# Statistics one tile ahead, earlier transposes, and the last output tile in three pieces, in a fused attention and feed-forward kernel

## The chip, the cores and the metric

The kernel runs on one core of a Trainium2 chip. The metric is the device time of one execution in microseconds (us). Before the change the median was 224.88 us (4 runs, 224.37 to 225.04). A profile shows the span of one execution, about 1.7 us shorter than its device time (223.4 against 225.12 for the profiled execution of the kernel before).

Names: PE is TensorE's matmuls and PEld its weight loads, DVE is VectorE, ACT ScalarE, POOL GpSimd, SP SyncE. "ACTq" and "SPq" are the sequencers of ACT and SP issuing DMAs. PSUM (psT in the profile) is where PE's results lie, in numbered banks, until another engine reads them.

## The reference, cut to what matters

```python
x  = A_x                                    # [1, 2048, 640], bf16
xn = (x - mean) / sqrt(var + 1e-5)          # layer norm over the 640 columns
q, k, v = split(xn @ wqkv)                  # 32 heads of 20
phi = lambda t: where(t > 0, t + 1, exp(t)) + 1e-6
kv, z = sum_s phi(k) v^T, sum_s phi(k)      # linear attention
s = (phi(q) kv / (phi(q) z + 1e-6)) @ wo
g = silu(relu(xn @ w1) @ w2)                # w1 is [640, 1728]
out = x + s * g
```

The rows come as 16 tiles of 128. Tiles 0 to 3 are transposed on PE after their mean is taken off; tiles 4 to 15 are normalised on VectorE and transposed by a DMA.

## The kernel before

A scheduler helper records operations per engine, in program order, and puts in the semaphore waits. So an engine runs its own list strictly in order, and an instruction that waits holds everything behind it. The parts that matter:

```python
def aggr(t):                                # statistics, then rsy = (var + eps)^-0.5 on POOL
    DVE: bn_aggr(mv[t], stats[t])
    POOL: rsv[t] = var + eps
    POOL: rsy[t] = rsv[t] ** -0.5
def LN_stats(t): bn(t, 0); bn(t, 1); aggr(t)
def LN_norm(t):                             # needs rsy[t]
    DVE: xn[t] = (xin[t] - mean[t]) * rsy[t]
    if t >= 4: SP: DMA transpose xn[t] -> xnT[t]
    if t + 8 < 16: SP: load tile t + 8
# K_mm(t): 10 PE matmuls into two PSUM banks, of xcT (t < 4) or xnT
# K_exp(t), K_relu(t): ACT evacuates the banks into slot t % 4 of ek
def K_fin(t):                               # frees the slot
    DVE: e = min(e, 1) + 1e-6
    DVE: pk[t] = e + r
# ... cut ...
# hidden blocks of the first 512 rows; K_mm(4) follows n = 5, K_mm(5) follows n = 7
for n in range(13):
    H_block(0, n)                           # 5 matmuls of 512 columns on PE, relu on ACT
    if n < 4:
        LN_norm(n + 4)
        if n < 3: LN_stats(n + 5)
    if n in (3, 4): K_fin(2 * n - 6); K_fin(2 * n - 5)
    if 4 <= n < 8: LN_norm(n - 4)
    # ... cut ...
    if n in {5: 4, 7: 5, 9: 6, 11: 7}:
        K_mm(t, 0); K_exp(t, 0); K_relu(t, 0); K_fin(t)     # all on banks 0 and 1
```

Two more pieces of the argument come later in the program. In the G phase, five blocks of 32 matmuls (`G_block`) use the bank pairs 0, 2, 0, 2, 4 in turn, and ACT copied each result to SBUF. Just ahead of those copies in ACT's list stand four DMA issues that load w2. At the end, each output tile is made from ten matmuls (`s_tile`), the gate `g = silu(...)` by ACT, a multiply and an add by VectorE, and a store; the last tile was done in two halves of 320 columns.

## Time and profile before

| what | value before | where it is read |
|---|---|---|
| device time, median | 224.88 us | the runs |
| PE busy | 97% of 223.4 us | page, part 1 |
| hole before K_mm(5) | PE free at 22.74, starts 24.48 | timeline of PE |
| VectorE waits for rsy | 5 waits, 5.0 us | waits |
| G phase, first matmul to first matmul after it | 112.33 to 134.31 = 21.98 us | timeline |
| gate end to last add, last add to span end | 1.71 and 2.41 us | timeline |

PE is the bound. The page of the kernel before, its head:

```profile
span 223.4 us, 3512 instructions
PE 216.8 (97%) x1442; PEld 133.8 (60%) x1442; DVE 115.0 (51%) x213; ACT 86.6 (39%) x142; POOL 45.9 (21%) x69
```

That is an average. The view by stretches says where PE is not full. Each line has the stretch, its length and the busy time of PE, PEld, DVE, ACT and POOL, each with its count; then the TensorE clock that was granted (1.00 is full speed), the DMA share and GB/s.

```profile
0.00:12.60 12.60, 11.15 (x93) 9.04 (x94) 6.61 (x22) 7.12 (x14) 3.74 (x15) 1.00 0.81 247
12.60:24.50 11.90, 10.32 (x54) 4.93 (x52) 8.65 (x23) 8.06 (x15) 5.52 (x11) 1.00 0.75 202
24.50:112.20 87.70, 87.70 (x480) 43.69 (x481) 68.94 (x108) 52.82 (x89) 33.31 (x43) 1.00 0.27 65
112.20:134.30 22.10, 22.02 (x162) 15.58 (x161) 0.00 (x0) 3.41 (x5) 0.00 (x0) 1.00 0.90 281
134.30:218.30 84.00, 84.00 (x650) 59.64 (x648) 29.26 (x58) 14.47 (x20) 3.30 (x1) 1.00 0.21 74
```

In the third and fifth stretch PE is busy all the time. The second has lost 1.6 us. VectorE's timeline there shows why (start, duration, engine, line and operation; the bracket is idle time before it and what ended it):

```profile
14.37 0.45 DVE L435 TENSOR_SCALAR reg<-reg,mv,rsy 128x640 bf16<-128x640 bf16 x1
...
16.86 0.45 DVE L435 TENSOR_SCALAR reg<-reg,mv,rsy 128x640 bf16<-128x640 bf16 x1 [1.00 <-POOL rsy L424]
...
19.34 0.45 DVE L435 TENSOR_SCALAR reg<-reg,mv,rsy 128x640 bf16<-128x640 bf16 x1 [1.00 <-POOL rsy L424]
...
21.82 0.45 DVE L435 TENSOR_SCALAR reg<-reg,mv,rsy 128x640 bf16<-128x640 bf16 x1 [1.00 <-POOL rsy L424]
...
22.54 0.49 DVE L530 TENSOR_TENSOR reg<-regE 128x640 bf16<-128x640 bf16 x1
```

L435 is `LN_norm`; three times it waits 1.00 us for POOL's rsy, whose statistics VectorE itself finished only just before. The first L530 is the end of K_fin(0), at 23.03. And PE, on the same clock:

```profile
20.58 2.32 PE L570 MATMUL psT<-regX,reg 128*128 128x512 bf16 x10
24.48 1.53 PE L495 MATMUL psT<-reg 128*128 128x320 bf16 x10 [1.58 <-ACT regE L512]
```

Ten matmuls of 512 columns take 2.16 us (0.216 each; the 2.32 printed includes a modelled end), so PE was free at 22.74. K_mm(5) needs banks 0 and 1, which K_exp(4) and K_relu(4) free; K_exp(4) needs slot 0 of `ek`, which K_fin(0) frees. ACT's timeline shows that K_exp(4) waited for it:

```profile
23.12 1.30 ACT L512 ACTIVATE regE<-psT 128x640 bf16<-128x640 f32 x2 [3.11 <-DVE reg L530]
```

The true hole is 1.74 us.

In the G phase ACT's queue is held by issuing w2. The timeline of the kernel before:

```profile
114.76 5.70 ACTq L780 DMA_DIRECT2D reg<-in_B_w_dram  x2
120.51 1.42 ACT L793 ACTIVATE reg<-psT 128x640 bf16<-128x640 f32 x2 [7.38 <-issue]
121.26 12.88 PEld L788 LDWEIGHTS psT<-reg 128*128 128x128 bf16 x96 [0.42 <-ACT reg L793]
```

The tail of the kernel before, with the gate (L868), the multiplies (L893) and the adds (L896):

```profile
218.58 0.70 ACT L868 ACTIVATE reg<-psT 128x640 bf16<-128x640 f32 x1 [5.54 <-PE psT L840]
219.38 0.49 DVE L893 TENSOR_TENSOR reg<-psT,reg 128x320 bf16<-128x320 f32 x1 [1.22 <-ACT reg L868]
219.91 0.33 DVE L896 TENSOR_TENSOR reg<-reg 128x320 bf16<-128x320 bf16 x1
220.15 0.48 DVE L893 TENSOR_TENSOR reg<-psT,reg 128x320 bf16<-128x320 f32 x1
220.67 0.32 DVE L896 TENSOR_TENSOR reg<-reg 128x320 bf16<-128x320 bf16 x1
```

### The profile page before, as it was taken

The page shows a single profiled execution, that of the slowest core. Times are in us where ns is not written, and L with a number is a line of the kernel's source. Part 1 is how long each engine was busy: PE and PEld are TensorE (multiplying, and loading weights), DVE is VectorE, ACT ScalarE, POOL GpSimd, SP SyncE. Part 2 cuts the span into 40 slices and gives each one's busy share as a digit, 9 for nine tenths or more (in the row PEclk, how much of TensorE's full clock was granted, in tenths as well). Part 3 has the DMA queues.
Part 4 walks back from the last instruction along what each step waited for, and adds up shares of the span by engine and source line. Part 5 has one row for each costly group of instructions (what it writes and reads, how often), then busy time and mean ns, then how long its engine had stood idle before and what let it go on. Part 6 is the DMA issues. An engine that isn't in the chain of part 4 may idle for free.

```text
span 223.4 us, 3512 instructions
## 1 busy us (share of the span) xinstructions
PE 216.8 (97%) x1442; PEld 133.8 (60%) x1442; DVE 115.0 (51%) x213; ACT 86.6 (39%) x142; POOL 45.9 (21%) x69
## 2 busy tenths in 40 slices
PE   8999799999999999999999999999999999999993
PEld 8655354555544555444466777677767776776672
DVE  4766996798649999783700002940424240412243
ACT  4585766656665576554412113232021102110211
POOL 2252631111041599950000005000000000000000
PEclk9999999999999999999999999999999999999999
DMA  6996389621001233000099969900010100001011
GB/s 178 283 339 130 87 248 140 190 44 29 3 1 29 59 94 115 0 0 3 11 204 321 341 245 369 323 12 3 29 59 32 59 29 32 29 29 59 3 59 60
DMA packets 27761, 23.91 MB, mean 107 GB/s; under 512 B 11873, under 2 KB 27105, under 8 KB 27745
## 3 DMA queue, kind: packets, MB, share of 16 engines
q1 hardware_dynamic: 24512, 19.50, 30.7%
q10 hardware_dynamic: 3232, 4.18, 5.4%
q8 instruction: 11, 0.18, 0.3%
q14 instruction: 6, 0.04, 0.1%
HBM read 15.81 MB, written 5.24 MB: 94 GB/s over the span
## 4 chain that ended last, share of the span: by engine, by line
PE 83%; DVE 4%; ACTq 3%; DMA 3%; SPq 2%; ACT 1%; POOL 1%; issue 1%; DVEq 0%
PE psT L840 25%; PE psT L570 21%; PE psT L548 10%; PE psT L879 9%; PE psT L495 7%; PE psT L788 6%; DMA reg<-in_A_x_dram 3%; ACTq L780 3%; DVE stats L416 2%; PE psT L817 1%; PE psT L858 1%; PE psT L587 1%; SPq L358 1%; ACTq L776 1%; POOL rsy L424 1%
## 5 line engine op out<-in xcount | busy, mean ns | idle before, releaser
L840 PE MATMUL psT<-reg,hT 128*128 128x320 bf16 x416 | 60.5, 299 | 0.0
L840 PEld LDWEIGHTS psT<-reg,hT 128*128 128x128 bf16 x416 | 40.3, 98 | 16.5 <-issue 1.1
L570 PE MATMUL psT<-reg 128*128 128x512 bf16 x195 | 46.0, 379 | 0.0
L893 DVE TENSOR_TENSOR reg<-psT,reg 128x640 bf16<-128x640 f32 (+1 forms) x17 | 13.3, 785 | 48.8 <-PE psT L879 47.6
L574 ACT ACTIVATE hT<-psT 128x512 bf16<-128x512 f32 x52 | 30.5, 601 | 17.4 <-PE psT L570 17.4
L570 PEld LDWEIGHTS psT<-reg 128*128 128x128 bf16 x195 | 18.9, 98 | 22.0 <-issue 0.4
L868 ACT ACTIVATE reg<-psT 128x640 bf16<-128x640 f32 x12 | 8.2, 702 | 43.1 <-PE psT L840 23.6
L548 PE MATMUL psT<-reg 128*128 128x512 bf16 x100 | 24.8, 379 | 0.0
L506 POOL TENSOR_TENSOR zacc<-zacc,reg 128x640 f32<-128x640 f32 x16 | 23.8, 1489 | 3.7 <-DVE reg L530 2.8
L879 PE MATMUL psT<-reg,pqT 128*128 128x320 bf16 x160 | 24.3, 299 | 0.0
L788 PE MATMUL psT<-reg 128*128 128x320 bf16 x160 | 22.1, 299 | 0.1
L512 ACT ACTIVATE regE<-psT 128x640 bf16<-128x640 f32 x24 | 15.6, 701 | 11.4 <-PE psT L495 8.3
L495 PE MATMUL psT<-reg 128*128 128x320 bf16 x120 | 18.3, 299 | 1.6 <-ACT regE L512 1.6
L788 PEld LDWEIGHTS psT<-reg 128*128 128x128 bf16 x160 | 15.6, 98 | 6.6 <-ACT reg L793 0.4
L879 PEld LDWEIGHTS psT<-reg,pqT 128*128 128x128 bf16 x160 | 15.7, 98 | 6.1
L556 DVE TENSOR_SCALAR regE<-psT 128x512 bf16<-128x512 f32 x20 | 13.6, 682 | 8.2 <-ACT regE L555 8.2
L558 DVE SCALAR_TENSOR_TENSOR pqT<-regE 128x512 bf16<-128x512 bf16 x20 | 17.4, 870 | 0.7
L548 PEld LDWEIGHTS psT<-reg 128*128 128x128 bf16 x100 | 9.8, 98 | 11.5
L495 PEld LDWEIGHTS psT<-reg 128*128 128x128 bf16 x120 | 11.7, 98 | 8.3 <-ACT regE L512 2.1
L416 DVE BATCH_NORM_STATS2 stats<-reg 128x6 f32<-128x320 bf16 x32 | 14.1, 479 | 3.3 <-DMA reg<-in_A_x_dram 3.3
L806 DVE TENSOR_TENSOR reg<-psT,mv 128x120 bf16<-128x120 f32 (+1 forms) x6 | 1.1, 261 | 27.9 <-POOL reg L910 27.9
L530 DVE TENSOR_TENSOR reg<-regE 128x640 bf16<-128x640 bf16 x16 | 14.5, 909 | 1.4 <-ACT regE L512 1.0
(68 smaller groups left out, 166.6 us busy)
## 6 DMA issues: line engine op xcount, KB each, us to landing
reg<-in_A_x_dram SPq DMA_DIRECT2D x16, 160.0 KB, 3.0
scr<-regE SPq DMA_DIRECT2D x4, 640.0 KB, 11.2
reg<-in_A_x_dram SPq DMA_DIRECT2D x4, 640.0 KB, 9.2
out_dram<-reg SPq DMA_DIRECT2D x15, 160.0 KB, 1.8
regE<-scr SPq DMA_DIRECT2D x4, 512.0 KB, 5.3
reg<-in_B_w_dram ACTq DMA_DIRECT2D x1, 1120.0 KB, 12.3
reg<-in_B_w_dram ACTq DMA_DIRECT2D x1, 1040.0 KB, 6.6
reg<-in_A_wo_dram SPq DMA_DIRECT2D x6, 160.0 KB, 4.2
```

Source lines behind the costliest of these rows:

```text
L416: sc.op("DVE", lambda eng: eng.bn_stats(stats[:, t, a, :], xv[:, HN * a:HN * (a + 1)]), R=[("xin", t % XR)], W=[("stats", t, a)])
L495: fns.append(lambda eng, a=a, k=k, lhs=lhs: eng.matmul(ps[b + a][:, 0:HN], lhsT=lhs[:, k, tok(t)], rhs=wqk[:, k, D + HN * a:D + HN * (a + 1)],
L506: sc.op("POOL", lambda eng: eng.tensor_tensor(out=zacc[:, :], in0=zacc[:, :], in1=pk[:, t, :], op=ALU.add), R=[("zacc",), ("pk", t)], W=[( ...
L512: sc.op("ACT", lambda eng: eng.activation(out=o_.rearrange("p (a n) -> p a n", a=2), in_=ps2(b, HN), func=func, scale=scale), R=[("ps", b) ...
L530: sc.op("DVE", lambda eng: eng.tensor_tensor(out=pk[:, t, :], in0=e_, in1=r_, op=ALU.add), R=[("ek_e", es), ("ek_r", es)], W=[("pk", t)])
L548: sc.group("PE", [(lambda eng, k=k: eng.matmul(ps[b], lhsT=wqk[:, k, P * f:P * (f + 1)], rhs=xnT[:, k, schunk(j)], start=(k == 0), stop=(k ...
L558: sc.op("DVE", lambda eng: eng.scalar_tensor_tensor(out=pqT[:, f, schunk(j)], in0=e_, scalar=1.0, in1=r_, op0=ALU.min, op1=ALU.add), R=[(" ...
L570: a = sc.group("PE", [(lambda eng, k=k: eng.matmul(ps[b], lhsT=w1_sb[:, k, P * f:P * (f + 1)], rhs=src[:, k, :], start=(k == 0), stop=(k = ...
L574: sc.op("ACT", lambda eng: eng.activation(out=hT[:, f, schunk(j)], in_=ps[b], func=ACTF.Relu), R=[("ps", b)], W=[("hT", j, f)])
L788: fns.append(lambda eng, t=t, a=a: eng.matmul(ps[b + a][:, 0:HN], lhsT=xn[:, t, P * k:P * (k + 1)], rhs=pk[:, t, HN * a:HN * (a + 1)], sta ...
L840: sc.group("PE", [(lambda eng, f=f: eng.matmul(ps[b][:, 0:HN], lhsT=hT[:, f, tok(t)], rhs=w2_sb[:, f, HN * n:HN * (n + 1)], start=(f == 0 ...
L879: sc.group("PE", [(lambda eng, c=c, a=a: eng.matmul(ps[b + a][:, 0:HN], lhsT=pqT[:, c, tok(t)], rhs=wf[:, c, HN * a:HN * (a + 1)], start=( ...
```

## The change

The intent is to keep PE fed at the opening, to take the rsy waits off VectorE, to free PSUM in the G phase sooner, and to overlap the last tile's work. There are four parts.

```diff
@@ opening @@
-    for k in range(KA, C):
-        K_mm(0, 2, k, k + 1)
-        K_mm(1, 4, k, k + 1)
     bn(1, 1)
     centre(2)
     aggr(1)
-    transposes(2, 0)
+    bn(2, 0)
     mean_act(3, 0)
-    bn(2, 0)
-    xcT_copy(2, 0, 0, "DVE")
-    xcT_copy(2, 0, 1, "DVE")
+    for k in range(KA, C):
+        if k == C - 1:
+            transposes(2, 0)
+            xcT_copy(2, 0, 0, "DVE")
+            xcT_copy(2, 0, 1, "DVE")
+        K_mm(0, 2, k, k + 1)
+        K_mm(1, 4, k, k + 1)
     # ... cut ...
-    bn(2, 1)
     xcT_copy(3, 0, 0, "DVE")
-    xcT_copy(3, 0, 1, "ACT")
+    xcT_copy(3, 0, 1, "DVE")
+    bn(2, 1)
     # ... cut ...
-    K_mm(3, 0)
+    K_mm(3, 0, 0, KA)
+    K_mm(3, 0, KA, C)
     K_exp(1, 4)
     K_relu(1, 4)
-    LN_stats(4)
     bn(3, 0)
     bn(3, 1)
     aggr(3)
+    LN_stats(4)
@@ first hidden blocks @@
                 if n < 4:
-                    LN_norm(n + 4)
                     if n < 3:
                         LN_stats(n + 5)
-                if n in (3, 4):
-                    K_fin(2 * n - 6)
-                    K_fin(2 * n - 5)
+                    LN_norm(n + 4)
+                if 1 <= n < 5:
+                    K_fin(n - 1)
@@ G_block @@
-        sc.op("ACT", lambda eng: eng.activation(out=GT[...], in_=ps2(b, HN), func=ACTF.Copy), ...)
+        sc.op("DVE", lambda eng: eng.tensor_copy(GT[...], ps2(b, HN)), ...)
@@ last output tile @@
+    LC = [0, 224, 432, 640]     # columns
+    LB = [2, 3, 4]              # PSUM banks
-    s_tile(pairs[7][1], 2, last=True)       # 320 + 320
+    s_last(pairs[7][1])                     # 224 + 208 + 208, each with its own mult, add and store
```

More of the change, by code (lines that the diff above doesn't have):

```diff
@@ L260, in bass_recurrent_scan__linear_attn_block__dense_activation_relu__prompt_kernel @@
     kvp = reg3[:, 0:VC * D].rearrange("p (c n) -> p c n", c=VC)
-    outb = reg3[:, VC * D:(VC + NOUT) * D].rearrange("p (a n) -> p a n", a=NOUT)
-    tmpo = reg3[:, (VC + NOUT) * D:(VC + 2 * NOUT) * D].rearrange("p (a n) -> p a n", a=NOUT)
+    NB = NOUT + 1
+    outb = reg3[:, VC * D:(VC + NB) * D].rearrange("p (a n) -> p a n", a=NB)
+    tmpo = reg3[:, (VC + NB) * D:(VC + 2 * NB) * D].rearrange("p (a n) -> p a n", a=NB)
     pqT = nc.alloc_sbuf_tensor("pqT", [P, C, S], bf)
@@ L632, in bass_recurrent_scan__linear_attn_block__dense_activation_relu__prompt_kernel @@
     K_mm(2, 6, KA, C, (1,))
+    xcT_copy(3, 0, 0, "DVE")
+    xcT_copy(3, 0, 1, "DVE")
     bn(2, 1)
-    xcT_copy(3, 0, 0, "DVE")
-    xcT_copy(3, 0, 1, "ACT")
     w1_load(2, "ACT")
@@ L792, in G_block @@
                       W=[("ps", b), ("ps", b + 1)])
-        sc.op("ACT", lambda eng: eng.activation(out=GT[:, k, :].rearrange("p (a n) -> p a n", a=2), in_=ps2(b, HN),
-                                                func=ACTF.Copy), R=[("ps", b), ("ps", b + 1)], W=[("GT", k)])
+        sc.op("DVE", lambda eng: eng.tensor_copy(GT[:, k, :].rearrange("p (a n) -> p a n", a=2), ps2(b, HN)),
+              R=[("ps", b), ("ps", b + 1)], W=[("GT", k)])
         return ag
@@ L872, in bass_recurrent_scan__linear_attn_block__dense_activation_relu__prompt_kernel, with s_out @@
     so = [0]
-    def s_tile(t, b, last=False):
+    LC = [0, 224, 432, 640]
+    LB = [2, 3, 4]
+    def s_out(t, os_, i, lo, hi, src, keys, na):
+        shp = "p (a n) -> p a n"
+        sc.op("DVE", lambda eng: eng.tensor_tensor(
+            out=tmpo[:, os_, lo:hi].rearrange(shp, a=na), in0=src, in1=g_sb[:, t, lo:hi].rearrange(shp, a=na),
+            op=ALU.mult), R=keys + [("g", t)], W=[("tmpo", os_, i)])
+        sc.op("DVE", lambda eng: eng.tensor_tensor(out=outb[:, os_, lo:hi], in0=tmpo[:, os_, lo:hi],
+                                                   in1=xre[:, t, lo:hi], op=ALU.add),
+              R=[("tmpo", os_, i), ("xre", t // 4)], W=[("outb", os_, i)])
+        dma("SP", lambda eng: eng.dma_start(out2[tok(t), lo:hi], outb[:, os_, lo:hi]), R=[("outb", os_, i)])
@@ L875, in s_tile, with s_mm @@
+    def s_mm(t, lo, hi, b):
+        i = t // 4
+        sc.group("PE", [(lambda eng, c=c: eng.matmul(
+            ps[b][:, 0:hi - lo], lhsT=pqT[:, c, tok(t)], rhs=wf[:, c, lo:hi],
+            start=(c == 0), stop=(c == C - 1))) for c in range(C)],
+            R=[("pqT", i, c) for c in range(C)] + [("wf", c) for c in range(C)], W=[("ps", b)])
+    def s_tile(t, b):
         os_ = so[0] % NOUT
         so[0] += 1
-        i = t // 4
         for a in range(2):
-            sc.group("PE", [(lambda eng, c=c, a=a: eng.matmul(
-                ps[b + a][:, 0:HN], lhsT=pqT[:, c, tok(t)], rhs=wf[:, c, HN * a:HN * (a + 1)],
-                start=(c == 0), stop=(c == C - 1))) for c in range(C)],
-                R=[("pqT", i, c) for c in range(C)] + [("wf", c) for c in range(C)], W=[("ps", b + a)])
@@ L884, in piece @@
-        def piece(lo, hi, pin, addE="DVE"):
-            shp = "p (a n) -> p a n"
-            na = 2 if pin is None else 1
-            src = ps2(b, HN) if pin is None else ps[pin][:, 0:HN].unsqueeze(1)
-            def kk(nm):
-                return [(nm, os_, h) for h in (0, HN) if lo <= h < hi]
-            keys = [("ps", b), ("ps", b + 1)] if pin is None else [("ps", pin)]
-            sc.op("DVE", lambda eng: eng.tensor_tensor(
-                out=tmpo[:, os_, lo:hi].rearrange(shp, a=na), in0=src, in1=g_sb[:, t, lo:hi].rearrange(shp, a=na),
-                op=ALU.mult), R=keys + [("g", t)], W=kk("tmpo"))
-            sc.op(addE, lambda eng: eng.tensor_tensor(out=outb[:, os_, lo:hi], in0=tmpo[:, os_, lo:hi],
-                                                      in1=xre[:, t, lo:hi], op=ALU.add),
-                  R=kk("tmpo") + [("xre", t // 4)], W=kk("outb"))
-            dma("SP", lambda eng: eng.dma_start(out2[tok(t), lo:hi], outb[:, os_, lo:hi]), R=kk("outb"))
@@ L901, in s_tile, with s_last @@
-        if last:
-            piece(0, HN, b)
-            piece(HN, D, b + 1)
-        else:
-            piece(0, D, None)
+            s_mm(t, HN * a, HN * (a + 1), b + a)
+        s_out(t, os_, 0, 0, D, ps2(b, HN), [("ps", b), ("ps", b + 1)], 2)
+    def s_last(t):
+        for i in range(3):
+            lo, hi = LC[i], LC[i + 1]
+            s_mm(t, lo, hi, LB[i])
+            s_out(t, NOUT, i, lo, hi, ps[LB[i]][:, 0:hi - lo].unsqueeze(1), [("ps", LB[i])], 1)
     lastG = None
```

## The prediction

> **What bounds the kernel now.** TensorE: the page gives PE 97% of 223.4 us at full granted clock; the chain of waits is 83% PE. The table of stretches shows PE busy 87.70 of 87.70 us in 24.5-112.2 and 84.00 of 84.00 in 134.3-218.3; moves inside those are worth nothing. The change can win only in the opening (0-12.6: 11.15 busy), the first hidden-layer blocks (12.6-24.5: 10.32 busy), a seam in the G phase, and the tail after 218.3.
>
> **Each part, costed.**
>
> 1. *Statistics one tile ahead, early K_fin: the main gain.* VectorE waits 1.0 us three times for GpSimd's rsy before a norm, so K_fin(0) ends only at 23.03. K_exp(4) needs its slot and waits 3.1 us; K_mm(5) needs K_exp(4)'s banks. The last hidden-layer matmul before K_mm(5) starts at 22.5 and streams 0.216 us, so PE is free at 22.74; K_mm(5) starts at 24.48. That is a hole of 1.74 us (the waits view shows 1.58, with modelled ends). After the change K_fin(0) should end near 17.5, long before K_mm(4) ends (20.3): gain 1.74.
>
> 2. *Transposes of tile 2 moved forward, copy of tile 3 to VectorE.* PE stalls about 0.3 us before K_mm(2) (a transpose weight load ends 9.00, the next load starts 9.39) and 0.35 before K_mm(3) (ScalarE's copy of 384 columns takes 491 ns; VectorE's 348 at most). Splitting K_mm(3) gains nothing: its first part writes both banks and waits for both copies. Estimate: the first hidden block starts 0.35 earlier.
>    Against it: VectorE gets more copying, and LN_norm(4) now follows the stats of tiles 3, 4 and 5; by my sum of durations it ends near 15.2 instead of 14.82. Its DMA transpose took 4.1 us and K_mm(4) began almost on its landing. PE gets there earlier and may wait: I charge 0.15.
>
> 3. *G evacuation on VectorE.* ScalarE is held issuing w2 loads from 112.9 to 120.5, so G's first copy ends 121.22 and the third G block starts late: 160 matmuls take 21.98 us against 21.78 at 0.1361. VectorE is idle there; a 128x640 f32 PSUM cast on it takes 825 ns (ScalarE 710), hidden. Gain 0.2.
>
> 4. *Last tile in three pieces.* The start is held by the gate activation (ends 219.28), unchanged. Then VectorE runs until 220.99. From the 640- and 320-column durations (820/490 and 490/330 ns) I estimate a fixed 0.15 us per instruction; two more make the last add end about 0.27 later. The last DMA carries less, but the Trainium skill ("DMA: Bandwidth & Descriptors", Specifications) says transfers below 512 B do read-modify-write, and pieces are 448 and 416 B per row, not 640; no run here shows that yet. Cost 0.25.
>
> **Sum.** 1.74 + 0.35 - 0.15 + 0.2 - 0.25 = 1.9 us, all on the critical path because PE is saturated afterwards. 224.86 - 1.9 gives 222.9 us, range 222.2 to 223.7. Faster by over 2%: 2%; within: 97%; slower: 1%.
>
> **What would show it.** K_mm(5)'s wait for K_exp (1.6 us) and VectorE's rsy waits gone; PE start of the second hidden stage (33.96 before) near 32.0; G phase near 21.8 us; last matmul to end of span longer by 0.2-0.3; K_mm(4) perhaps waiting for a DMA transpose.
>
> **What would make it wrong.** Tile 4's or 5's input landing later because the w1 load on ScalarE's queue starts about 1 us sooner while DMA is saturated (286 GB/s in 4-11 us); earlier zacc adds on GpSimd slowing VectorE's K_fin adds (0.49 us alone, 1.6 beside them) until another PE hole opens; or the tail shorter with small pieces.

## The result, and the profile after

The kernel after takes 223.28 us (4 runs, 223.05 to 223.65) against 224.88 us. The ratio is 0.9934, with a 95% interval of 0.9913 to 0.9956: 1.5 us of 224.8. Ratios are the mean time of one kernel's runs over that of the other's runs of the same rounds, so they are not quite the ratio of the quoted medians. Executions over 1.5% slower than the fastest of the same kernel are left out of the means. The time lies inside the predicted range of 222.2 to 223.7, and 0.4 us above its point estimate of 222.9. It is also within the 2% to which the prediction gave 97%.

The page of the kernel after:

```profile
span 221.3 us, 3515 instructions
PE 215.9 (98%) x1437; PEld 134.2 (61%) x1447; DVE 119.2 (54%) x221; ACT 82.9 (37%) x136; POOL 46.9 (21%) x69
```

The spans differ by 2.1 us, more than the times do. The profiled execution of after was the fastest of its four (their spans are 221.3, 221.6, 221.5 and 221.9), and the profiled one of before took 225.12 us, longer than each of the four timed ones (224.37 to 225.04). So the traces are read for which wait is gone, and the timed rounds for what it was worth.

VectorE after, in the same place. L436 is the norm, L531 the end of K_fin:

```profile
14.80 0.45 DVE L436 TENSOR_SCALAR reg<-reg,mv,rsy 128x640 bf16<-128x640 bf16 x1
...
16.20 0.40 DVE L436 TENSOR_SCALAR reg<-reg,mv,rsy 128x640 bf16<-128x640 bf16 x1
16.51 0.32 DVE L529 TENSOR_SCALAR regE<-regE 128x640 bf16<-128x640 bf16 x1
16.86 0.49 DVE L531 TENSOR_TENSOR reg<-regE 128x640 bf16<-128x640 bf16 x1
...
19.93 1.51 DVE L436 TENSOR_SCALAR reg<-reg,mv,rsy 128x640 bf16<-128x640 bf16 x1 [0.46 <-POOL rsy L425]
```

The three brackets of 1.00 are gone: the statistics of the next tile fill the time in which POOL makes rsy. K_fin(0) ends at 17.35, not 23.03. The prediction had all rsy waits gone, and that is not so: the waits view still has three, 2.5 us in all. One is the last line above: there only one norm and K_fin(1) stand between the tile's statistics and its norm. That norm also takes 1.51 us, not 0.40 to 0.45, beside GpSimd's zacc adds, which now run from 19.86 to 22.73; the prediction had named such a slowing as a risk. Both come after K_fin(0), and no hole of PE opened. PE after:

```profile
20.43 2.32 PE L571 MATMUL psT<-regX,reg 128*128 128x512 bf16 x10
22.59 1.52 PE L496 MATMUL psT<-reg 128*128 128x320 bf16 x10
```

20.43 + 2.16 = 22.59, so K_mm(5) follows without a gap. In the stretch that had lost 1.6 us PE is now busy 11.80 of 11.90 us:

```profile
12.60:24.50 11.90, 11.80 (x63) 6.17 (x63) 11.15 (x25) 8.83 (x15) 9.07 (x14) 1.00 0.81 203
```

In the G phase, PE runs straight through, and VectorE's casts lie beside it:

```profile
110.42 21.90 PE L790 MATMUL psT<-reg 128*128 128x320 bf16 x160
112.87 5.05 ACTq L782 DMA_DIRECT2D reg<-in_B_w_dram  x2
114.97 0.82 DVE L795 CAST reg<-psT 128x640 bf16<-128x640 f32 x1 [6.83 <-PE psT L790]
...
132.16 1.93 PE L842 MATMUL psT<-reg,hT 128*128 128x320 bf16 x13
```

132.16 - 110.42 = 21.74 us; it was 21.98. The tail of after, with the gate (L870), multiplies (L881) and adds (L884):

```profile
216.42 0.70 ACT L870 ACTIVATE reg<-psT 128x640 bf16<-128x640 f32 x1 [5.54 <-PE psT L842]
217.22 0.39 DVE L881 TENSOR_TENSOR reg<-psT,reg 128x224 bf16<-128x224 f32 x1 [1.22 <-ACT reg L870]
217.65 0.28 DVE L884 TENSOR_TENSOR reg<-reg 128x224 bf16<-128x224 bf16 x1
217.84 0.37 DVE L881 TENSOR_TENSOR reg<-psT,reg 128x208 bf16<-128x208 f32 x1
218.24 0.27 DVE L884 TENSOR_TENSOR reg<-reg 128x208 bf16<-128x208 bf16 x1
218.43 0.36 DVE L881 TENSOR_TENSOR reg<-psT,reg 128x208 bf16<-128x208 f32 x1
218.83 0.27 DVE L884 TENSOR_TENSOR reg<-reg 128x208 bf16<-128x208 bf16 x1
```

From the gate's end (217.12) to the last add's end (219.10) it is 1.98 us, against 1.71 before.

Following one point after another through both traces: the first hidden block's weight load moves by -0.15 us (12.61 to 12.46), K_mm(5) by -1.89 (24.48 to 22.59), the first G matmul by -1.91, the first matmul after G by -2.15 (134.31 to 132.16), the last add by -1.89 (220.99 to 219.10), the end by -2.1. The second hidden stage starts at 32.06 instead of 33.96; the prediction had it near 32.0.

### The profile page after: what moved, and what is told of

Same layout as the page of the kernel before. It is cut to its first block, busy times and chain, and to the rows that moved or that the text cites. A ratio compares the mean times of both kernels' runs of the same rounds, so it can differ in the third digit from the quotient of the medians.

```text
span 221.3 us, 3515 instructions
## 1 busy us (share of the span) xinstructions
PE 215.9 (98%) x1437; PEld 134.2 (61%) x1447; DVE 119.2 (54%) x221; ACT 82.9 (37%) x136; POOL 46.9 (21%) x69
## 3 DMA queue, kind: packets, MB, share of 16 engines
q10 hardware_dynamic: 3232, 4.18, 5.3%
## 4 chain that ended last, share of the span: by engine, by line
PE 93%; DMA 2%; SPq 2%; DVE 1%; issue 1%; ACT 0%; ACTq 0%; DVEq 0%
PE psT L842 26%; PE psT L571 25%; PE psT L790 10%; PE psT L549 10%; PE psT L891 9%; PE psT L496 8%; DMA reg<-in_A_x_dram 2%; PE psT L819 1%; PE psT L860 1%; PE psT L588 1%; SPq L359 1%; PE psT L805 1%; SPq L340 1%; PE psT L677 1%; DVE reg L881 0%
## 5 line engine op out<-in xcount | busy, mean ns | idle before, releaser
L571 PE MATMUL psT<-reg 128*128 128x512 bf16 x192 | 45.5, 379 | 0.3 <-issue 0.2
L881 DVE TENSOR_TENSOR reg<-psT,reg 128x640 bf16<-128x640 f32 (+2 forms) x18 | 13.5, 750 | 48.8 <-PE psT L891 47.6
L870 ACT ACTIVATE reg<-psT 128x640 bf16<-128x640 f32 x12 | 8.2, 702 | 43.1 <-PE psT L842 23.6
L891 PE MATMUL psT<-reg,pqT 128*128 128x320 bf16 (+2 forms) x165 | 24.4, 295 | 0.0
L549 PE MATMUL psT<-reg 128*128 128x512 bf16 x95 | 23.8, 379 | 0.3
L870 ACT ACTIVATE reg<-psT,rsy 128x640 bf16<-128x640 f32 x4 | 3.2, 794 | 38.6 <-PE psT L860 33.4
L795 DVE CAST reg<-psT 128x640 bf16<-128x640 f32 x5 | 4.1, 824 | 20.9 <-PE psT L790 20.9
L556 ACT ACTIVATE regE<-psT 128x512 bf16<-128x512 f32 x20 | 12.0, 598 | 8.5 <-PE psT L549 8.5
```

The lines of the kernel that those rows point to most:

```text
L549: sc.group("PE", [(lambda eng, k=k: eng.matmul(ps[b], lhsT=wqk[:, k, P * f:P * (f + 1)], rhs=xnT[:, k, schunk(j)], start=(k == 0), stop=(k ...
L571: a = sc.group("PE", [(lambda eng, k=k: eng.matmul(ps[b], lhsT=w1_sb[:, k, P * f:P * (f + 1)], rhs=src[:, k, :], start=(k == 0), stop=(k = ...
L881: sc.op("DVE", lambda eng: eng.tensor_tensor(out=tmpo[:, os_, lo:hi].rearrange(shp, a=na), in0=src, in1=g_sb[:, t, lo:hi].rearrange(shp, a ...
L891: sc.group("PE", [(lambda eng, c=c: eng.matmul(ps[b][:, 0:hi - lo], lhsT=pqT[:, c, tok(t)], rhs=wf[:, c, lo:hi], start=(c == 0), stop=(c = ...
```

## The experiments

Eleven kernels ran, all correct, each timed beside the kernel before over five rounds. The first four ran in one job, the next four in a second, the last three in a third. The effects of most parts are smaller than the scatter of single executions (the kernel before ranged from 224.08 to 226.11 in the first job).

| kernel | median us | ratio to before (95%) |
|---|---|---|
| b_stats | 223.57 | 0.9944 (0.9918 to 0.9970) |
| b_kfin | 223.75 | 0.9962 (0.9928 to 0.9996) |
| b_open | 226.43 | 1.0066 (1.0039 to 1.0092) |
| b_G | 225.00 | 1.0008 (0.9984 to 1.0032) |
| b_tail | 225.26 | 0.9992 (0.9953 to 1.0032) |
| a_two | 223.74 | 0.9935 (0.9904 to 0.9967) |
| a_x3 | 223.50 | 0.9919 (0.9886 to 0.9952) |
| a_half | 222.58 | 0.9877 (0.9845 to 0.9908) |
| b_open2 | 224.86 | 1.0004 (0.9965 to 1.0042) |
| a_noopen | 223.44 | 0.9927 (0.9908 to 0.9945) |
| a_half2 | 222.53 | 0.9886 (0.9868 to 0.9905) |

Names with b_ start from the kernel before, those with a_ from the kernel after. The median of before was 224.79, 225.23 and 225.21 us in the three jobs.

The following table was read from the timelines of all profiles. "Tile 3" is when ScalarE starts its mean of input tile 3, right as the tile lands (in a_x3 the tile was there before). "Stats 4" is when VectorE starts tile 4's statistics. "H" is the first weight load of the hidden blocks, "K5" that of K_mm(5). A weight load that nothing holds runs about 0.2 us ahead of its matmul (22.37 and 22.59 in after; 24.47 and 24.48 in before), so K5 - H falls by 1.95 us where PE's hole was 1.74.

| kernel | tile 3 | stats 4 | H | K5 | K5 - stats 4 | K5 - H |
|---|---|---|---|---|---|---|
| before | 8.30 | 12.24 | 12.61 | 24.47 | 12.23 | 11.86 |
| b_G | 10.05 | 12.26 | 13.63 | 24.48 | 12.22 | 10.85 |
| b_tail | 9.89 | 12.09 | 13.47 | 24.32 | 12.23 | 10.85 |
| b_open | 9.60 | 13.34 | 13.08 | 25.50 | 12.16 | 12.42 |
| b_open2 | 9.02 | 12.72 | 12.50 | 24.95 | 12.23 | 12.45 |
| b_stats | 8.84 | 12.56 | 12.81 | 22.72 | 10.16 | 9.91 |
| b_kfin | 8.23 | 12.15 | 12.50 | 22.41 | 10.26 | 9.91 |
| after | 8.99 | 12.72 | 12.46 | 22.37 | 9.65 | 9.91 |
| a_two | 9.50 | 13.23 | 12.97 | 22.89 | 9.66 | 9.92 |
| a_noopen | 9.67 | 12.12 | 13.25 | 23.16 | 11.04 | 9.91 |
| a_x3 | 6.85 | 13.04 | 12.78 | 22.74 | 9.70 | 9.96 |
| a_half | 8.49 | 12.37 | 12.02 | 21.88 | 9.51 | 9.86 |
| a_half2 | 8.67 | 12.47 | 12.15 | 22.35 | 9.88 | 10.20 |

In the first five kernels K_mm(5) starts 12.2 us after tile 4's statistics, whatever PE does: H varies by 1.1 us and K_mm(5) doesn't follow it. In the other eight K_mm(5) starts 9.9 to 10.0 us after H, while its distance from VectorE's statistics runs from 9.51 to 11.04; only a_half2 has 10.20, because PE lost about 0.3 us there waiting for K_mm(4)'s transpose. The limit has changed from VectorE's chain to PE's own work.

### b_stats: only the statistics ahead of the norm

```diff
-                    LN_norm(n + 4)
                     if n < 3:
                         LN_stats(n + 5)
+                    LN_norm(n + 4)
```

> Kernel before with one part of the change: statistics of the next tile before the norm of this one, K_fin left where it was. Theory: the 1.74 us hole before K_mm(5) exists only because K_fin(0) ends at 23.03, after K_mm(4) ends (about 20.4); anything that ends K_fin(0) before about 20.6 closes it whole. Without rsy waits K_fin(0) should end near 20.1: hole 1.6 to 0.0-0.2 in the waits view, total 1.5 to 1.7 us shorter. Rival: the two edits each own a share of the hole, so this one alone closes about half (0.8 to 1.0 us).

The wait of K_mm(5) on K_exp is gone from its waits view, and K5 - H is 9.91. K_fin(0) ended at 20.66 (expected near 20.1; one rsy wait of 0.77 us in front of it is left), late but still in time. The total is 0.56% or about 1.3 us shorter, below the expected 1.5 to 1.7, though its interval (0.7 to 1.8 us) holds that.

### b_kfin: only the earlier K_fin

```diff
-                if n in (3, 4):
-                    K_fin(2 * n - 6)
-                    K_fin(2 * n - 5)
+                if 1 <= n < 5:
+                    K_fin(n - 1)
```

> Kernel before with the other part alone: K_fin(0) to K_fin(3) one per hidden block from the second on, statistics order left. Theory: VectorE keeps its three 1.0 us rsy waits, but K_fin(0) ends near 19.2, before K_mm(4) ends; the hole closes whole, total 1.5 to 1.7 us shorter, the same as the statistics order alone. Rival: shares, about half each.

The hole is closed as completely here (K5 - H is 9.91). K_fin(0) ended at 18.95 (expected near 19.2). VectorE's five rsy waits are still there, though with 3.9 us in all and not 5.0, since K_fin now fills part of two of them. So the two edits do not own shares; either alone does the whole job at K_mm(5), and there the rival falls. The total does not decide it: it is about 0.85 us shorter, which looks like a half, and its interval (0.1 to 1.6 us) reaches both forecasts. The trace of the profiled execution shows where 0.5 us of the rest went. PE's waits in b_kfin have a new line:

```profile
PE psT L495 <- DMA reg<-reg: 0.5, 1, 0.5
```

It is K_mm(8) in the second 512 rows, waiting for its DMA transpose. SP's timeline of b_kfin:

```profile
27.87 3.36 SPq L339 DMA_DIRECT2D reg<-in_A_x_dram  x4
31.28 7.66 SPq L486 DMA_TRANSPOSE reg<-reg  x5
```

SP issues four tile loads and five DMA transposes back to back until 38.94. The norm of tile 8 was ready at 36.86, but the last transpose, 1.2 us of issue, started near 37.74; 2.6 us later, at 40.34, PE started K_mm(8). In after the same list of SP starts at 25.72 and is not late. Closing one hole thus uncovered the next, half a microsecond long.

### b_open: only the reordered opening

The edit is the first part of the diff above.

> Kernel before with the reordered opening alone. Theory: the first hidden block starts 0.15 to 0.35 us earlier, but the hole before K_mm(5) is set by VectorE's chain to K_fin(0), which does not end earlier, so the hole grows by as much and the total stays within 0.2 us. Rival: the opening's gain carries through, total 0.15 to 0.35 us shorter, hole unchanged at 1.6.

Neither held: the opening alone is 0.66% or 1.5 us slower, and clear of noise. The table shows tile 4's statistics 1.10 us later than in before (13.34 against 12.24) and K_mm(5) with them. The waits view of b_open has one rsy wait more than before (6.0 us in 6, not 5.0 in 5), and it is the norm of tile 4, which waits bare because its own statistics are now right in front of it. VectorE's timeline of b_open:

```profile
13.34 0.83 DVE L416 BATCH_NORM_STATS2 stats<-reg 128x6 f32<-128x320 bf16 x2
14.21 0.21 DVE L420 BATCH_NORM_AGGREGATE mv<-stats 128x2 f32<-128x12 f32 x1
15.41 0.45 DVE L435 TENSOR_SCALAR reg<-reg,mv,rsy 128x640 bf16<-128x640 bf16 x1 [0.99 <-POOL rsy L424]
```

In before, tile 3's statistics stood between tile 4's statistics and its norm and covered that wait. From tile 4's statistics to its norm it is 2.13 us in before and 2.07 us here, so that distance has not grown; what is lost is the 0.99 us that tile 3's statistics now take in front. In before VectorE had idled 1.17 us at that place, waiting for tile 4 to land. In b_open tile 3 landed late (9.60), and VectorE came to these statistics too late to use such idle time. Whether the order costs as much when tile 3 lands early was not measured.

### b_open2: the opening, with tile 4's statistics back in front

```diff
+    LN_stats(4)
     bn(3, 0)
     bn(3, 1)
     aggr(3)
-    LN_stats(4)
```

(relative to b_open)

> The opening alone, but with tile 4's statistics put back before tile 3's, as in the kernel before. Theory: the opening alone was slower because the norm of tile 4 then followed its own statistics directly and VectorE waited for GpSimd's rsy once more (6.0 us in 6 waits, not 5.0 in 5), which moved K_fin(0) and K_mm(5) by 1.0 us; put back, rsy waits are 5 again, K_mm(5) starts at 24.3 to 24.7 and the total is within 0.3 us of before. Rival: the loss comes from the copies on VectorE or from the earlier w1 load, and K_mm(5) still starts near 25.5.

The loss is gone: 1.0004, with five rsy waits again. K_mm(5) started at 24.95, outside the expected 24.3 to 24.7, because tile 4 landed late and its statistics started at 12.72; the distance is again 12.23. The copies on VectorE and the earlier w1 load are in this kernel too, so they are not the cause. In the full change tile 4's norm starts without a wait (14.80, shown above), as tile 5's statistics stand between, and K_fin(0) ends about 3 us before K_mm(4) does. (The profiled execution of b_open2 was its slowest, 227.55 us at a granted clock of 0.992; of its trace after 26 us only the hold of ACT and the landing of the last store are used, below.)

### b_G: only the G copies on VectorE

```diff
-        sc.op("ACT", ... activation(out=GT, in_=ps2(b, HN), func=ACTF.Copy))
+        sc.op("DVE", ... tensor_copy(GT, ps2(b, HN)))
```

> Kernel before with only the G evacuation moved to VectorE. Theory: the 160 G matmuls go from 21.98 to 21.74 us and everything behind is 0.24 us earlier; VectorE's casts stay hidden. Rival: the casts on VectorE delay the kv products or the divides and open a PE gap after 134, total unchanged or longer.

The G phase took 21.74 us (112.33 to 134.07), as expected, and no later PE gap opened. The timing (1.0008) is too coarse for 0.24 us. But the other profiles show that 0.24 is not a constant. With the copies on ACT, G took 21.73 in b_stats and b_kfin, 21.74 in b_open, 21.98 in before and 22.37 in b_tail. The difference is how long ACT was held by issuing w2: 7.08, 7.09, 7.10, 7.38 and 7.76 us. The two blocks that PE can do meanwhile are worth 64 x 0.136 = 8.7 us; a short hold fits in, a long one doesn't. In b_open2, at its lower clock, the hold was 7.63 us and PE stalled for 0.33. b_tail's PE:

```profile
121.49 13.21 PE L789 MATMUL psT<-reg 128*128 128x320 bf16 x96 [0.46 <-ACT reg L794]
```

With the copies on VectorE, G took 21.73 or 21.74 us in every profile. So this part gains between 0 and 0.6 us, and it takes away a source of scatter.

### b_tail: only the last tile in three pieces

The edit is the last part of the diff above, with the fifth output buffer.

> Kernel before with only the last tile in three pieces. Theory: VectorE's chain after the gate ends 0.27 us later (six instructions instead of four), the last DMA (52 KB instead of 80 KB) lands about 0.2 us sooner, together +0.06 us: no gain. Rival: three pieces shorten the tail because the last DMA is small, total 0.2 us or more shorter.

The gate's end to the last add is 1.98 us (219.50 to 221.48), 0.27 more than in before, and the last add to the end is 2.32 us; gate end to span end is 4.30 us, against 4.12. The total is unchanged within its interval, which runs from 1.1 us shorter to 0.7 us longer and so cannot exclude the rival's 0.2 us. VectorE's extra instructions are certain; for the landing see the next run.

### a_two: after, with two pieces of 432 and 208

```diff
-    LC = [0, 224, 432, 640]
-    LB = [2, 3, 4]
+    LC = [0, 432, 640]
+    LB = [2, 3]
```

> Kernel after with two pieces of 432 and 208 columns instead of three. Theory: two instructions' fixed cost (0.27 us) comes back and the last DMA stays as small as with three, so last add to end is as after and the tail from gate end to span end is 0.2 to 0.27 us shorter than after. Rival: the shorter landing of after came from the queue, not from the size, and the tail ends as in after or before.

This missed. VectorE's part is 0.15 us shorter than with three pieces (1.83 us), because the first multiply now waits for more matmuls, and the last add to the end took 2.54 us, not 2.20. Over the eleven profiles in which the whole last tile stands behind the gate, last add to end was 2.33 to 2.62 us with a last store of 80 KB (six, mean 2.47) and 2.13 to 2.54 us with 52 KB (five, mean 2.34); in the last two kernels below it was 1.96 us with 40 KB and 2.10 us with 80 KB. So the 0.2 us by which the landing seemed to improve in after is inside the scatter, and I withdraw size as its cause.

### a_x3: after, with tile 3 loaded before three weight loads

```diff
     x_load(2)
+    x_load(3)
     for k in range(KA, C):
         wk_load(k)
-    x_load(3)
```

> Kernel after with the load of input tile 3 issued before the last three K weight loads. Theory: in after the opening was held by that tile's landing at 8.96 (PE idle 0.3 us before its transposes, again before K_mm(3)); landing 1 us earlier, the first hidden block should start about 0.3 us earlier (12.1 to 12.2) and, unless K_mm(4) waits for its DMA transpose, the total is 0.2 to 0.3 us shorter. Rival: the K weights now land late and PE stalls in K_mm(0) and K_mm(1): no gain.

The rival was right about the opening. ScalarE got to tile 3 at 6.85, two microseconds earlier, yet H started at 12.78, later than in after. PE's weight loads waited 0.4 us for the K weights and 0.97 us before the third slice of K_mm(0) instead (the view names a VectorE centring there that this group does not need; it probably was the third weight slice), and K_mm(4)'s weight load waited 0.37 us for its transpose, of which PE lost under 0.1 us. The total is not distinguishable from after. The opening needs four tiles and five weight slices of 160 KB each before K_mm(3) can end, and in this run the other order only moved the stall.

### a_noopen: after, with the opening of before

The edit is the first part of the diff, undone.

> Kernel after with the opening of before (the rest of the change kept). Theory: the opening's order is worth 0.1 to 0.2 us, less than the scatter of tile 3's landing (8.2 to 10.1 us over the profiles so far), so the total is 0 to 0.3 us longer than after: ratio to before 0.993 to 0.996. Rival: the prediction's 0.35 us or more: ratio 0.996 or above.

The ratio is 0.9927 (0.9908 to 0.9945), just below the expected 0.993 to 0.996, against 0.9934 of after in another job: no loss that can be seen, and the rival's 0.996 is outside the interval. The table offers a reason. When tile 3 lands late, the old opening starts H 3.58 us after it (b_G, b_tail, a_noopen) and the new one 3.47 or 3.48 us after it (after, a_two, b_open, b_open2), a gain of 0.11 us. The landing itself ranged from 8.23 to 10.05. When tile 3 lands early the old order does have a floor (before and b_kfin: H 4.3 us after it; b_stats, at 8.84: 3.97 us), so then the new one can gain more; a_half, at 8.49, started H at 12.02.

### a_half: the last gate split, half of the last tile before the last hidden product

```diff
+    def gate_half(t, b, n):
+        ACT: g[t, half n] = silu(ps[b + n])
-    LC = [0, 224, 432, 640]
+    LC = [0, 320, 480, 640]
     # for the last tile:
     U_sub(7, 1, 0)
+    gate_half(0)              # runs while PE does the second half
     s_of(7, 0, 0)
+    s_last(piece 0)           # 320 columns
     U_sub(7, 1, 1)
-    gate(7, 1)
-    s_last(pieces 0, 1, 2)
+    gate_half(1)
+    s_last(pieces 1, 2)       # 160 + 160
```

> Kernel after with the last gate split into halves (the first runs while PE computes the second half) and the last tile's first 320 columns multiplied by PE before the last hidden product, then 160 and 160. Theory: after the last PE matmul only one mult and one add of 160 columns and a DMA are left, so the last add ends about 0.8 us earlier relative to the last hidden product than in after, total 0.6 to 0.8 us shorter. Rival: the smaller last DMA (320 B rows) or a PE wait on the new order gives it back.

This beats both kernels: 222.58 us, ratio 0.9877 (0.9845 to 0.9908), whose interval does not touch that of after (0.9913 to 0.9956). The kernel after itself was not in that job; the two other variants of it there, with the long tail, had 223.74 and 223.50 us, so the gain is 0.9 to 1.2 us (expected 0.6 to 0.8). The end of a_half:

```profile
217.19 0.44 ACT L909 ACTIVATE reg<-psT 128x320 bf16<-128x320 f32 x1 [3.37 <-PE psT L842]
217.73 0.32 DVE L881 TENSOR_TENSOR reg<-psT,reg 128x160 bf16<-128x160 f32 x1 [0.87 <-ACT reg L909]
218.09 0.24 DVE L884 TENSOR_TENSOR reg<-reg 128x160 bf16<-128x160 bf16 x1
218.25 0.32 DVE L881 TENSOR_TENSOR reg<-psT,reg 128x160 bf16<-128x160 f32 x1
218.60 0.24 DVE L884 TENSOR_TENSOR reg<-reg 128x160 bf16<-128x160 bf16 x1
```

From the start of the last gate to the span's end it is 3.61 us (217.19 to 220.8), against 4.88 in after (216.42 to 221.3). Of those 1.27 us, 0.68 are five matmuls (5 x 0.136) that moved to before the gate; 0.59 us are gained. Of these, 0.35 us lie ahead of the last add (1.65 us from the gate's start, against 2.68, less the 0.68) and 0.24 us are a quicker landing (1.96 us against 2.20), which is within what landings scatter. Its opening gained 0.44 us more at H, but K_mm(8) then waited 0.42 us for its transpose, behind SP's list as in b_kfin. So that gain was not kept.

### a_half2: the same with 320 columns in the last piece

```diff
-    LC = [0, 320, 480, 640]
+    LC = [0, 320, 640]
```

> The split-gate tail with the last 320 columns in one piece. Theory: VectorE's chain behind the last half gate is 0.25 us shorter, the last DMA of 80 KB instead of 40 KB lands 0.1 to 0.2 us later; last hidden matmul to span end within 0.15 us of the split-gate run with 160 and 160. Rival: the piece count rules, 0.25 us shorter.

The last gate's start to the end is 3.63 us (217.07 to 220.7), against 3.61 with two pieces, as expected, and the time is 222.53 us. In this job each of its five executions (222.34 to 223.29) was below each of the six of a_noopen, which has the long tail (223.33 to 224.24). The piece count does not matter here. What does is one or both of the two things that a_half changed, the split gate and the half tile moved ahead of it; no run separates them.

## Why the prediction was right

- **The hole before K_mm(5), 1.74 us: right.** K_mm(5) moved by 1.89 us and H by 0.15, so 1.74 is the hole itself. K_fin(0) was put at "near 17.5" and ended at 17.35. What the prediction did not see is that either edit alone would have done, and that 2.5 us of rsy waits would stay, after K_fin(0).
- **The opening, 0.35 us less 0.15 for K_mm(4)'s transpose: the net came out by luck, its terms did not.** H moved 0.15 us in the profiled pair, and PE did not wait for that transpose in after (it did in a_half2, for about 0.3 us). The mis-sized term is "the first hidden block starts 0.35 earlier". It took tile 3's landing of 8.30 for given; in after it was 8.99, and with late landings the reorder is worth 0.11 us. The stall before K_mm(2) went, but PE then waited 0.47 us for tile 3's centring, and K_mm(3)'s weight load still waits 0.41 us for a copy, against 0.51 in before. In timed rounds it is worth nothing that can be seen (a_noopen).
- **The G copies, 0.2 us: right for this pair (0.24), but not a constant:** 0 to 0.6 us, by the length of ACT's hold.
- **The tail, "cost 0.25": VectorE's part was right to the hundredth (0.27 us), the whole was +0.06 us** from gate end to span end (4.12 to 4.18). The Trainium skill's page "VectorE: DVE Perf Modes", in its section on the TRN2 errata, has an fp32 tensor_tensor add at (N+151)/0.96 ns, measured there at 512 and 2048 columns. Carried over to the multiplies of this tail, which read fp32 from PSUM and bf16 from SBUF, that gives as an estimate 824, 491 and 374 ns for 640, 320 and 208 columns. The traces agree (0.82, 0.49 and 0.37 us), and two halves cost 0.16 us more than one whole (2 x 0.49 - 0.82) for the multiply alone. The rest is landing scatter of up to half a microsecond, which no run here ties to the size of the store. The Trainium skill's page "DMA: Bandwidth & Descriptors", Specifications, says that transfers below 512 B do read-modify-write; with rows of 416 B the end was no later (mean 2.34 us) than with 640 B (2.47 us), and with rows of 320 B, in a_half, it was 1.96 us, so no cost of it shows here.
- **The sum: 1.9 predicted, 1.5 measured** (ratio), 1.6 by the medians, 2.1 by the two traces. The traces' part adds up: 1.74 + 0.15 + 0.24 - 0.06 = 2.07 us. "All on the critical path because PE is saturated afterwards" holds for this trace, but with less reserve than the words say: b_kfin and a_half lost 0.5 and 0.4 us again at K_mm(8). I did not trace each timed execution, so how the remaining 0.4 us divides among landing, K_mm(8) and tail stays open.

The parts do not add. Measured alone they sum to about -0.65 us (-1.3, -0.85, +1.5, +0.2 and -0.2, the last two within noise), and together they give -1.5: two close the same hole, and the opening, harmful alone, did no harm that can be seen in after (a_noopen).

## What to carry to other kernels

Before costing a reorder, look for which of two engines' chains sets the next start, and test it by the differences of starts across several runs: the difference that stays constant names the limit, as 12.2 us from tile 4's statistics and 9.9 us from the first hidden block did here. When an in-order engine needs a result that another engine makes from its own output, put other work between the two; and after moving one piece of work, check what it used to cover. Split the last operation so that only what depends on the last product stands behind it, rather than into more pieces behind the same wait.

## What the Trainium skill lacked or had wrong

- "DMA: Bandwidth & Descriptors", Issuing engines are not separate DMA queues, calls the sequencer's issue time "usually small relative to the DMA itself". Here ACT's four w2 issues held its compute for 7.08 to 7.76 us, long enough to stall PE in three of the six profiles that have the copies on ACT (before, b_tail, b_open2), though each issue (0.37 to 3.49 us in before) was still short beside its own landing (12.3 to 16.2 us). Apart from a count of cycles per instruction for "previous generations", the page has no figure for how long issues hold an engine, nor for its scatter.
- The same page gives bandwidths for DMA transposes, but no time to landing for a single 128x640 bf16 tile within SBUF: here 2.6 us at the least, with 1.20 us of issue on SP (up to 4.1 us to landing in before and 4.8 us in after). Eight issues ahead of one transpose in SP's queue made K_mm(8) late.
- "SBUF — State Buffer", SBUF: two separate sides, describes a pair of ports shared by VectorE and GpSimd that one of them holds for a whole instruction. The traces agree: K_fin's add takes 0.49 us alone, and 1.57 to 1.62 us beside GpSimd's 1.4 us zacc add. The page has no durations for these two instructions; here it was off the critical path.
